# Two of the six model-column blocks of the first tile's layer 1 computed in one pass of 512 tokens instead of two passes of 256

## The chip, the core and the metric

One NeuronCore of one Trainium2 chip runs the whole program. The metric is the device time of one execution in microseconds (us), as a median of several runs. The engines are named as in the profile: PE (TensorE matmul), PEld (its weight loads), DVE (VectorE), ACT (ScalarE), POOL (GpSimd) and SP (the queue that issues most DMAs).

## What is computed

The reference has three stages, each feeding the next. Only what matters here is kept:

```python
y = _attn_ref(x, a, B, C)        # a chunked decay attention: batch 4, 8 heads, 768 tokens, head dim 32
x = y.transpose(0, 2, 1, 3).reshape(3072, 256)
h = np.maximum(np.maximum(x @ w1, x @ w2), x @ w3)      # layer 1: 256 -> 768
x = h @ w_out                                           # 768 -> 256
h = x @ w_in                                            # layer 2: 256 -> 2048
g = np.maximum(h, 0.0) + alpha * np.minimum(h, 0.0)
out = g @ w_out2                                        # 2048 -> 256
```

## The kernel before

**Tokens.** The 3072 tokens form 24 blocks of 128 (block r) and six tiles of 512 (tile t = blocks 4t to 4t+3). Attention is done block by block, the two layers tile by tile, and attention for later blocks is spread between the matmuls of the layers.

**Units.** The work of a layer is cut into units. One unit of layer 1 is one block f of 128 of the 768 hidden columns, over a number of tokens. `up1` (L664 to L682) makes three products (j = 0, 1, 2, for w1, w2, w3). Each is six matmuls (L652) into one of three PSUM buffers called `up`, because every operand is held as a high and a low part: two steps of the contraction, times high by high, low by high and high by low. ACT moves the first product out (L676), DVE takes the maximum with the second and the third (L678). ACT then makes the high part gh (L137) and POOL the low part gl (L138). The unit's way down (`down`, matmuls `acc<-gh,wo` and `acc<-gl,wo`, six in all) comes two units later (LAG = 2). A unit of layer 2 has one product of six matmuls, two DVE steps out of PSUM (L690, L691), then gh, gl and six matmuls down (`acc<-gh,vo`, `acc<-gl,vo`).

**Order of the phases.** Tile 0 layer 1, tile 1 layer 1, tile 0 layer 2, tile 2 layer 1, tile 1 layer 2, and so on. Tile 0's layer 1 is the first phase. Its units are taken in halves of 256 tokens, so that it can begin when attention blocks 0 and 1 are there:

```python
SPLIT, WHOLE = ((0, 256), (256, 256)), ((0, 512),)
ORDER = [(0, 0), (1, 0), (0, 1), (1, 1), (2, 0), (2, 1)]
        cut = [(f, *tokens[h]) for q, h in ORDER for f in (2 * q, 2 * q + 1)]
```

A pair (q, h) stands for the column blocks 2q and 2q+1 on token piece h of SPLIT. So the units are, in order: blocks 0 to 3 on tokens 0 to 255 (units 0 to 3), blocks 0 to 3 on tokens 256 to 511 (units 4 to 7), blocks 4 and 5 on tokens 0 to 255 (units 8 and 9), blocks 4 and 5 on tokens 256 to 511 (units 10 and 11). From unit 4 on all four attention blocks of tile 0 are done. Units 12 to 17 are tile 1's layer 1, units 18 to 33 tile 0's layer 2.

**Attention between the units.** A list `todo` of small steps is handed out at a rate (`quota`) worked out from the columns left until the next tile needs its blocks. For block r the steps on PE are: `att_t` (transposes, L400), `att_b` (products of C and B, L478, later L468), `att_y` (the output, L552 and L560) and `att_u` (the state, L511). ACT makes the decay matrix e by exponentials (`att_e`, L456) from a DMA of sums (`e<-cum_d`, L350), POOL masks it (L459), DVE multiplies it by the result of `att_b` (L483). The result of `att_y` goes into the next layer's input, high part by ACT (L569), low part by DVE (L570). Tile 1's first matmul needs block 7. In this text y7 means `att_y` of block 7, and so on.

**Weights.** 28 pieces of weights arrive by DMA (L163) and are turned from 64-bit words into two parts in four steps each, 112 steps in all: DVE L177, DVE L179, ACT L183, and DVE L185, which also lets ACT rebias the next piece (L170). In the first phase each unit hands out four such steps (pace 1). Afterwards `quota_w` spreads what is left over the units until the weights are needed.

**What orders the instructions.** In the first phase a scheduler of the language orders each engine's instructions. From tile 1 on (STRICT = 1) they stand in the order in which the program writes them. On every engine instructions are executed in order.

Of the kernel before, what the change touches and what calls it, by code (L numbers as in the profile page):

```python
# [27 lines left out]
NF1, NF2 = FF1 // P, FF2 // P  # L28
NT = BT * S // 512

SPLIT, WHOLE = ((0, 256), (256, 256)), ((0, 512),)
LATE = 4
PHASES = [(1, 0, SPLIT, 1), (1, 1, WHOLE, 0)]
for _t in range(NT - 2):
# [20 lines left out]
NPA = 2  # L55
SUMS = 0
WIDE = 18
ORDER = [(0, 0), (1, 0), (0, 1), (1, 1), (2, 0), (2, 1)]
BW, KW = 1, 3
WARM = 8  # L60
IDLE = 2
# [22 lines left out]
def fused(ctx: ExitStack, tc: tile.TileContext, x, a, B, C, w1, w2, w3, w_out, v_in, v_out, alpha, cst, out):  # L84
# [535 lines left out]
    def units_of(ph):  # L620
# [4 lines left out]
        else:  # L625
            cut = [(f, *tokens[h]) for q, h in ORDER for f in (2 * q, 2 * q + 1)]
        return [(f, o, n, (24 if layer == 1 else 12) * n, (4 * t + (o + n) // P) * (layer == 1),
# [494 lines left out]
```

## Time and profile before

| | us |
|---|---|
| median of 3 runs | 541.57 |
| lowest, highest | 541.23, 543.72 |
| profiled execution: its own time | 540.72 |
| profiled execution: span of its instructions | 539.0 |

The profile is of one execution. Its span runs from the first instruction to the last, and 1.72 us lie around it. Times in its rows are counted from the start of the span.

### The profile page before, as it was taken

What the parts mean: (1) busy time and instruction counts of PE and PEld (TensorE: products, weight loads), DVE (VectorE), ACT (ScalarE), POOL (GpSimd) and SP (SyncE); (2) the same over time, 40 slices, a digit from 0 to 9 for tenths busy, and PEclk for the clock granted to TensorE, in tenths of its full rate; (3) what the DMA queues carried; (4) which work ended last, traced back from release to release, by engine and by line L of the source; (5) the groups of instructions that cost most, each with busy time, mean ns of one, the idle gap of its engine ahead of it and who ended that gap; (6) DMA issues with size and microseconds to landing.
All of it is one profiled execution on the core that took longest, in us unless ns stands there. A gap on an engine that the chain in (4) does not pass through costs nothing.

```text
span 539.0 us, 9568 instructions
## 1 busy us (share of the span) xinstructions
PE 527.4 (98%) x3402; PEld 427.1 (79%) x3403; DVE 341.4 (63%) x596; ACT 254.1 (47%) x610; POOL 242.3 (45%) x267
## 2 busy tenths in 40 slices
PE   8898999999999999999999999999999999999997
PEld 4777888787788888888788888888877888778886
DVE  5887886789984547665347566345845736775453
ACT  6677774664653342432433424424242234766551
POOL 2143453443763433654433645422553352885550
PEclk9999999999999999999999999999999999999999
DMA  8978796687753762535663644634220200000024
GB/s 153 231 149 187 181 189 167 156 219 173 200 109 75 158 122 62 134 73 99 129 135 66 131 96 88 137 75 119 48 64 2 39 1 0 1 0 1 1 40 119
DMA packets 209344, 55.60 MB, mean 103 GB/s; under 512 B 159632, under 2 KB 201168, under 8 KB 209296
## 3 DMA queue, kind: packets, MB, share of 16 engines
q1 hardware_dynamic: 206928, 54.46, 45.9%
q10 hardware_dynamic: 2368, 0.52, 0.4%
q8 instruction: 27, 0.44, 0.4%
q14 instruction: 21, 0.17, 0.1%
HBM read 44.35 MB, written 10.62 MB: 102 GB/s over the span
## 4 chain that ended last, share of the span: by engine, by line
PE 82%; DVE 7%; ACT 3%; issue 3%; DMA 2%; POOL 1%; SPq 1%; ACTq 0%; DVEq 0%; POOLq 0%
PE up L652 43%; PE acc L652 27%; PE at L652 5%; PE at L539 1%; DVE v L179 1%; PE at L468 1%; POOL gl L138 1%; DVE g L678 1%; DMA xm<-in_x_dram 1%; PE at L536 1%; SPq L247 1%; DMA e<-cum_d 1%; PE up L977 1%; ACT e L451 1%; PE at L478 1%
## 5 line engine op out<-in xcount | busy, mean ns | idle before, releaser
L138 POOL TENSOR_TENSOR gl<-g,gh 128x512 fp32r<-128x512 f32 (+1 forms) x109 | 136.6, 1253 | 218.0 <-ACT gh L137 207.6
L652 PE MATMUL up<-xt,w 128*128 128x512 f32 (+1 forms) x777 | 168.5, 364 | 1.1 <-ACT xt L569 0.6
L137 ACT ACTIVATE gh<-g 128x512 fp32r<-128x512 f32 (+1 forms) x114 | 69.4, 609 | 186.3 <-DVE g L691 101.8
L652 PEld LDWEIGHTS up<-xt,w 128*128 128x128 f32 x777 | 132.5, 188 | 26.6 <-issue 2.2
L652 PE MATMUL up<-yt,vi 128*128 128x512 f32 x459 | 117.0, 389 | 0.0
L678 DVE TENSOR_TENSOR g<-up,g 128x512 f32<-128x512 f32 (+1 forms) x84 | 51.3, 611 | 77.2 <-PE up L652 75.6
L652 PEld LDWEIGHTS up<-yt,vi 128*128 128x128 f32 x459 | 86.0, 188 | 17.9
L652 PE MATMUL acc<-gh,vo 128*128 128x512 f32 x268 | 83.9, 394 | 0.0
L690 DVE TENSOR_SCALAR g<-up,alph 128x512 f32<-128x512 f32 x64 | 47.8, 747 | 38.0 <-PE up L652 36.3
L652 PEld LDWEIGHTS acc<-gh,vo 128*128 128x128 f32 x268 | 49.1, 188 | 10.4 <-issue 0.4
L652 PE MATMUL acc<-gl,vo 128*128 128x512 f32 x134 | 52.4, 391 | 0.2
L652 PE MATMUL acc<-gh,wo 128*128 128x512 f32 (+1 forms) x168 | 47.2, 365 | 0.3 <-ACT gh L137 0.2
L691 DVE SCALAR_TENSOR_TENSOR g<-up,g 128x512 f32<-128x512 f32 x64 | 44.3, 692 | 2.2
L451 ACT ACTIVATE e<-e,ncum 128x128 f32<-128x128 f32 x120 | 38.0, 388 | 0.0
L676 ACT ACTIVATE g<-up 128x512 f32<-128x512 f32 (+1 forms) x42 | 22.4, 534 | 27.1 <-PE up L652 16.3
L652 PEld LDWEIGHTS acc<-gh,wo 128*128 128x128 f32 x168 | 29.7, 189 | 6.1 <-DVE yt L719 0.5
L652 PE MATMUL acc<-gl,wo 128*128 128x512 f32 (+1 forms) x84 | 30.2, 360 | 0.0
L652 PEld LDWEIGHTS acc<-gl,vo 128*128 128x128 f32 x134 | 25.2, 188 | 6.4 <-POOL gl L138 1.0
L179 DVE SCALAR_TENSOR_TENSOR v<-st,v 128x512 uint32<-128x512 uint32 x28 | 24.6, 879 | 2.3 <-ACT st L170 0.7
L452 POOL TENSOR_SCALAR_AFFINE_SELECT e<-e 128x512 f32<-128x512 f32 x30 | 19.8, 659 | 7.9 <-ACT e L451 7.9
L170 ACT ACTIVATE st<-st 128x512 f32<-128x512 f32 x28 | 18.8, 671 | 2.0 <-DMA st<-in_moe_w_in_dram 1.0
L867 DVE SCALAR_TENSOR_TENSOR g<-g,rest,up 128x512 f32<-128x512 f32 x16 | 11.9, 747 | 11.9 <-ACT g L866 11.6
(192 smaller groups left out, 658.6 us busy)
## 6 DMA issues: line engine op xcount, KB each, us to landing
e<-cum_w SPq DMA_DIRECT2D x30, 256.0 KB, 4.4
st<-sc SPq DMA_DIRECT2D x60, 128.0 KB, 2.5
sc<-ts SPq DMA_DIRECT2D x52, 112.0 KB, 2.4
st<-in_moe_w_out_dram SPq DMA_DIRECT2D x11, 512.0 KB, 5.7
st<-in_moe_w_dram SPq DMA_DIRECT2D x9, 512.0 KB, 4.9
st<-in_moe_w_in_dram SPq DMA_DIRECT2D x8, 512.0 KB, 5.0
v<-sc SPq DMA_DIRECT2D x60, 64.0 KB, 2.2
out_dram<-st SPq DMA_DIRECT2D x20, 128.0 KB, 3.0
```

The lines of the kernel that those rows point to most:

```text
L137: nc.scalar.activation(dst_h, src, AF.Copy)
L138: engine.tensor_tensor(dst_l, src, dst_h, ALU.subtract)
L170: nc.scalar.activation(hi, hi, AF.Prelu, scale=2.0 ** -112, alpha=2.0 ** 32)
L179: nc.vector.scalar_tensor_tensor(v, hi, 3, v, ALU.logical_shift_left, ALU.bitwise_or)
L451: nc.scalar.activation(e[:, q, :], e[:, q, :], AF.Exp, bias=ncum[:, k, b, 4 * g + q:4 * g + q + 1])
L452: nc.gpsimd.affine_select(out=e, in_=e, pattern=[[0, 4], [1, P]], compare_op=ALU.is_ge, fill=0.0, base=0, channel_multiplier=-1)
L652: nc.tensor.matmul(acc, w, r, start=(first and i == 0), stop=(last and i == len(todo_) - 1), skip_group_check=True)
L676: nc.scalar.activation(g, p, AF.Copy)
L678: nc.vector.tensor_tensor(g, p, g, ALU.max)
L690: nc.vector.tensor_scalar(g, p, 0.0, alph[:, f:f + 1], ALU.min, ALU.mult)
L691: nc.vector.scalar_tensor_tensor(g, p, 0.0, g, ALU.max, ALU.add)
L867: nc.vector.scalar_tensor_tensor(g, g, rest[:, f:f + 1], h, ALU.mult, ALU.add)
```

## The change

```diff
-SPLIT, WHOLE = ((0, 256), (256, 256)), ((0, 512),)
+SPLIT, WHOLE = ((0, 256), (256, 256), (0, 512)), ((0, 512),)
-ORDER = [(0, 0), (1, 0), (0, 1), (1, 1), (2, 0), (2, 1)]
+ORDER = [(0, 0), (1, 0), (0, 1), (1, 1), (2, 2)]
```

Column blocks 4 and 5 of tile 0 become two units of 512 tokens (units 8 and 9 of the changed kernel) in place of four of 256. The first phase then has ten units, and tile 1's layer 1 is units 10 to 15, tile 0's layer 2 units 16 to 31. With two units fewer, the first phase hands out 40 weight steps in place of 48. The instructions that do not belong to these blocks stay the same, but several stand elsewhere.

The first place is on PE, behind the way down of unit 6. There `att_b` of block 6 (L478) and the transposes of block 7 (L400) stand. Names: `xt_304` and `xt_305` are tile 0's input, high and low. Before:

```order
L478 MATMUL at<-bc 64x128 x8
L400 MATMUL at<-ct,b 128x128
L400 MATMUL at<-ct,c 128x128
L400 MATMUL at<-ct,cp 128x128
L652 MATMUL up<-xt_304,w_0_112 128x256 x2
L652 MATMUL up<-xt_304,w_1_113 128x256 x2
L652 MATMUL up<-xt_305,w_0_112 128x256 x2
```

Now:

```order
L478 MATMUL at<-bc 64x128 x8
L400 MATMUL at<-ct,b 128x128
L400 MATMUL at<-ct,c 128x128
L400 MATMUL at<-ct,cp 128x128
L552 MATMUL at<-cpt,u 64x64 x2
L560 MATMUL at<-e,xm_108 32x64 x5
L552 MATMUL at<-cpt,u 64x64 x2
L560 MATMUL at<-e,xm_108 32x64 x11
L652 MATMUL up<-xt_304,w_0_112 128x512 x2
```

Before, all 18 matmuls up of unit 9 and six down of unit 7 stood between these transposes and y6 (L552, L560). Now y6 follows directly, and the unit's matmuls come behind it.

The second place is on PE, at the end of the first phase, behind y7. `xt_947` and `xt_948` are tile 1's input. Before:

```order
L552 MATMUL at<-cpt,u 64x64 x8
L560 MATMUL at<-e,xm_109 32x64 x16
L511 MATMUL at<-xm_110,bp 32x128 x4
L652 MATMUL up<-xt_304,w_0_112 128x256 x2
L652 MATMUL up<-xt_304,w_1_113 128x256 x2
L652 MATMUL up<-xt_305,w_0_112 128x256 x2
```

Now:

```order
L552 MATMUL at<-cpt,u 64x64 x8
L560 MATMUL at<-e,xm_109 32x64 x16
L511 MATMUL at<-xm_110,bp 32x128 x4
L652 MATMUL up<-xt_947,w_0_112 128x512 x2
L652 MATMUL up<-xt_947,w_1_113 128x512 x2
L652 MATMUL up<-xt_948,w_0_112 128x512 x2
```

Before, a whole unit of tile 0 (unit 11), six matmuls down and `att_b` of block 8 stood between u7 (L511) and tile 1's first matmul. Now tile 1's first matmul is next, and `att_b` of block 8 comes 12 matmuls after it.

The third place is on ACT, at the same time: the exponentials of block 8 (L456) and the copies of y7 (L569). Before:

```order
L137 ACTIVATE gh<-g 128x256
L569 ACTIVATE xt_947<-at 128x128
L456 ACTIVATE e<-e,ncum 128x64 x8
L569 ACTIVATE xt_947<-at 128x128
L676 ACTIVATE g<-up 128x256
```

Now:

```order
L456 ACTIVATE e<-e,ncum 128x64 x7
L137 ACTIVATE gh<-g 128x512
L456 ACTIVATE e<-e,ncum 128x64
L569 ACTIVATE xt_947<-at 128x128 x2
L676 ACTIVATE g<-up 128x512
```

Both copies of y7 now stand behind all eight exponentials of block 8 and behind unit 9's gh.

On SP the sums of block 8 (`e<-cum_d`) are now issued ahead of a weight piece that came before them. From tile 1 on a few attention steps stand up to one unit later than before, and otherwise the order of PE is the old one to the end of the program.

## Rows read from the trace of the kernel before

**Rows 1.** The page: span, part 1 (busy us, share, instructions), part 4 by engine.
```profile
span 539.0 us, 9568 instructions
PE 527.4 (98%) x3402; PEld 427.1 (79%) x3403; DVE 341.4 (63%) x596; ACT 254.1 (47%) x610; POOL 242.3 (45%) x267
PE 82%; DVE 7%; ACT 3%; issue 3%; DMA 2%; POOL 1%; SPq 1%; ACTq 0%; DVEq 0%; POOLq 0%
```

**Rows 2.** Busy time by stretch: length, PE, PEld, DVE, ACT, POOL, clock, DMA.
```profile
62.80:82.90 20.10, 19.24 (x315) 16.85 (x313) 17.54 (x44) 15.91 (x55) 10.36 (x16) 1.00 0.85 174
82.90:118.20 35.30, 35.19 (x241) 28.21 (x238) 26.87 (x45) 21.27 (x52) 13.15 (x18) 1.00 0.72 185
...
124.00:156.00 32.00, 31.81 (x161) 25.32 (x160) 30.94 (x49) 15.53 (x35) 17.05 (x16) 1.00 0.65 162
```

**Rows 3.** Timeline of PE, units 8 to 11: start, length, instructions.
```profile
62.80 0.52 PE L652 MATMUL up<-xt,w 128*128 128x256 f32 x3
...
78.40 0.65 PE L560 MATMUL at<-e,xm 128*32 128x64 f32 x32
78.87 0.40 PE L511 MATMUL at<-xm,bp 128*32 128x128 f32 x8
79.20 2.42 PE L652 MATMUL up<-xt,w 128*128 128x256 f32 x18
81.46 0.40 PE L652 MATMUL acc<-gh,wo 128*128 128x256 f32 x2
...
81.82 0.40 PE L652 MATMUL acc<-gh,wo 128*128 128x256 f32 x2
...
82.27 0.67 PE L478 MATMUL at<-bc 64*64 64x128 f32 x16
82.87 4.42 PE L652 MATMUL up<-xt,w 128*128 128x512 f32 x18
```

**Rows 4.** The chain that ended last, in order of time: 18 matmuls of 512.
```profile
166.61 4.08 PE up L652 x18
```

**Rows 5.** Timeline, all engines: b6, its product with e, y6, b7.
```profile
67.84 0.67 PE L478 MATMUL at<-bc 64*64 64x128 f32 x16
...
69.09 0.74 DVE L483 TENSOR_TENSOR e<-at,e 128x256 f32<-128x256 f32 x2
...
71.78 0.34 PE L552 MATMUL at<-cpt,u 32*64 32x64 f32 x8
...
74.83 0.85 PE L478 MATMUL at<-bc 64*64 64x128 f32 x16 [0.75 <-DVE xt L570]
```

**Rows 6.** Timeline of SP and ACT: DMA issues up to block 8's sums, its exponentials.
```profile
68.83 2.24 SPq L233 DMA_DIRECT2D b<-in_B_dram  x1
...
73.78 1.12 SPq L350 DMA_DIRECT2D e<-cum_d  x2
...
79.41 2.10 ACT L456 ACTIVATE e<-e,ncum 128x64 f32<-128x64 f32 x8 [0.23 <-DMA e<-cum_d]
81.41 0.26 ACT L569 ACTIVATE xt<-at 128x128 fp32r<-128x128 f32 x1
```

**Rows 7.** Weight steps: L179 (ns min/median/max); L177, L185 by shape, 118 to 160 us.
```profile
L179 DVE SCALAR_TENSOR_TENSOR v<-st,v x28: 676/693/1610, 10.1 to 152.9; 128x512 uint32<-128x512 uint32 x28
...
L177 DVE TENSOR_SCALAR v<-st 128x512 uint32<-128x512 uint32 x6 | 3.1, 510 | 0.0
L185 DVE TENSOR_TENSOR vi<-v,vi 128x512 fp32r<-128x512 f32 x3 | 2.3, 776 | 0.0
```

**Rows 8.** Tile 0's layer 2: weight loads down with idle, one gl and its matmul.
```profile
L652 PEld LDWEIGHTS acc<-gl,vo 128*128 128x128 f32 x24 | 4.5, 188 | 1.9 <-POOL gl L138 1.0
...
130.31 1.30 POOL L138 TENSOR_TENSOR gl<-g,gh 128x512 fp32r<-128x512 f32 x1 [2.47 <-ACT gh L137]
...
131.67 0.50 PE L652 MATMUL acc<-gl,vo 128*128 128x512 f32 x1
```

## The prediction

> **What bounds the kernel now.** I first read the page. PE is busy for 527.4 of 539.0 us, and 82% of the chain that ended last lies on PE [rows 1]. So time is won where PE does less or waits less, and an engine beside it counts only where PE waits for it. The change acts in the stretch of units 8 to 11, 62.80 to 82.90 us of the span, so I read the busy time by stretch next. PE is busy for 19.24 of 20.10 us there, and DVE with 17.54 us and ACT with 15.91 us have 2.5 and 4.2 us to spare [rows 2]. Two later stretches get weight steps that the first phase gives up. In tile 1's layer 1 (82.90 to 118.20) DVE is busy for 26.87 of 35.30 us. In tile 0's layer 2 (124 to 156) it is busy for 30.94 of 32.00 us, which is 97%, while PE hardly waits [rows 2]. There DVE is nearly a second bound.
>
> Then I read PE's timeline for the places where work for attention and work for the layers meet, and the timelines of ACT and SP beside it [rows 3, 5, 6]. They show which distances on PE hide something now.
>
> **Part 1: fewer, wider matmuls.** Four units of 24 matmuls over 256 columns become two units of 24 over 512. In the row of unit 11, the 18 matmuls up start at 79.20 and the next instruction at 81.46: 2.26 us, 125.6 ns each. Of the way down, three start from 81.46 to 81.82, 120 ns each [rows 3]. At 512 columns 18 take 4.08 us, 226.7 ns each [rows 4]. So 72 x 125.6 + 24 x 120 = 11.92 us become 48 x 226.7 = 10.88 us: **-1.04 us**. If all the narrow ones took 120 ns it would be 11.52 - 10.88 = -0.64 us. I take -1.04, since unit 11 is one of the units that go.
>
> A rule speaks against this term. The Trainium skill, page "TensorE: Matmul & The Clock Gate", section "Back-to-back issue gap", gives the distance of isolated matmuls at full clock as columns over 2.4 GHz plus about 2.5 ns. By it two of 256 need only some 2.5 ns more than one of 512, and this part would give about 0.1 us (an estimate from that page). The rows differ: they show 240 to 251 ns for two of 256 against 226.7 ns, so I keep the term from the rows.
>
> Fused moves out of PSUM and fused gh and gl save some DVE, ACT and POOL time. I cost this at nothing, since these engines have spare time in that stretch [rows 2] and PE doesn't wait for these steps: way down comes two units later.
>
> **Part 2: y6 directly behind att_b of block 6.** Now 3.94 us of PE's work lie between the start of b6 (67.84) and y6 (71.78), mostly unit 9 up. DVE's product, which y6 needs, starts 1.25 us and ends 1.99 us after the start of b6 [rows 5]. In the new order only b6 and the three transposes, about 0.9 us, lie between. If DVE were as quick as now, PE would wait about 1.1 us. In the new DVE order a maximum over 512 and an L179 (0.69 us at the median [rows 7]) stand ahead of the product, behind the same matmuls. I take **+1.2 us**. Bounds: 0.3 us, if DVE is free and only its 0.74 us for the product counts against part of the transposes, and 2.2 us, if a long L179 (1.61 us [rows 7]) falls there. Behind the waiting y6 stand unit 9 and with it all of PE.
>
> **Part 3: the wait at b7.** PE waits there 0.75 us for the copies of y6 to free PSUM [rows 5]. In the new order the same work lies between y6 and b7 (u7 and six matmuls, now twice as wide, in place of u7 and eight), and five exponentials stand ahead of the copies on ACT. I leave it as it is: **0**, from -0.75 (gone) to +0.9 (it doubles).
>
> **Part 4: tile 1's first matmul directly behind u8.** Now from 79.20 to 82.87 unit 11, six matmuls down and b8 lie between the end of att_u of block 8 and tile 1, 3.67 us [rows 3]. They hide the copies of y7, and even a detour: the second copy (81.41) waits behind the eight exponentials of block 8 (2.10 us), and these wait for a DMA that lets them start at 79.41 [rows 6]. In the new order none of that cover is left; the hidden work is done after tile 1's first matmuls instead, so only the wait counts. When is PE there? Now u8 ends at 79.20 [rows 3]. Up to that point the new order has 36 wide matmuls up and 12 narrow ones down, 9.60 us, in place of 54 and 18 narrow ones, 8.94 us: 0.66 us more. With the 1.2 us of part 2, y7 ends at about 80.7 and u8 at 81.0. The exponentials need block 8's sums. Their DMA is issued at 73.78 [rows 6]. In the new order it goes ahead of a weight piece, but behind the load of b for block 9, which waits for the transposes of block 7 (68.83 now, behind L400), and these come 1.7 us later. The two nearly cancel, and the load of b took 2.24 us to issue anyway [rows 6]. If the exponentials start near 78 us, they and gh (0.6 us) are done by 80.8, and the copies of y7, two on ACT of 0.26 us each [rows 6], end at about 81.4. So PE waits **+0.4 us**. Bounds: 0 (ACT is early and u8 covers the copies) and +3.4 us (below, the rival).
>
> **Part 5: eight weight steps later.** Steps done when tile 0's layer 2 is through with them stay 112. Working the shares through `quota_w`, tile 1's layer 1 hands out 27 steps instead of 23 and the first twelve units of layer 2 27 instead of 23. Four steps are one piece: L177 0.51 + L179 0.69 + L185 0.78 = 2.0 us of DVE [rows 7]. In tile 1's layer 1 DVE has 8.4 us to spare [rows 2], so **0** there, up to +1. In layer 2 it has 1.06 us to spare between 124 and 156. Already now PE's weight loads stand idle for 1.0 us for gl [rows 8], as at 131.67, when PE starts 0.06 us after gl has ended (130.31 + 1.30) [rows 8]. gl follows gh, and gh DVE's two steps. So up to 2.0 us of DVE may reach PE. Early units get little of it, and in between there is slack of one to two us at other units. I take **+0.7 us**, from 0 to 2.0.
>
> Of L179 the row shows 676 to 1610 ns, with a median of 693 [rows 7]. The Trainium skill, page "SBUF — State Buffer", section "Who interferes with whom", says that a DVE instruction with two SBUF inputs and a GpSimd instruction that reads SBUF block each other for the whole instruction. By that rule an L179 that meets a gl on POOL takes the long time, which agrees with the maximum of that row. At 1.61 us a piece would cost 2.9 us of DVE, and the upper bound of this part would be 2.9 us.
>
> **Sum.** -1.04 + 1.2 + 0 + 0.4 + 0 + 0.7 = **+1.3 us**. The profiled execution took 540.72 us (539.0 of span and 1.72 around it), so the new one would take about 542.0. The median of the three runs, 541.57, stands 0.85 above it, and by it the forecast is **542.9 us**, +0.24%.
>
> **Rivals.**
>
> *Nothing new waits.* DVE and ACT have 40 steps to do in place of 48 in the first phase, they keep up, and only part 1 counts, with 0.64 to 1.04 us: 540.5 to 540.9. For it: DVE's spare 2.5 us in that stretch [rows 2]. Against it: the 1.99 us from b6 to the end of the product [rows 5] cannot fit in 0.9 us. Chance 0.20.
>
> *The lighter first phase removes waits.* All of PE's 20.10 - 19.24 = 0.86 us idle in that stretch [rows 2] goes too, with part 1 and nothing of the rest: -1.9, 539.7. If the 1.0 us of waits for gl in layer 2 [rows 8] went as well, it would be -2.9, 538.7. For it: 8 steps less on DVE and ACT. Against it: y6 has lost its cover. Chance 0.09.
>
> *Slower: the sums of block 8 land late and tile 1 waits for them.* Place: ACT, L456 ahead of L569. If the DMA slips by the 1.7 us of the transposes, the exponentials start at 81.1, end at 83.2, gh follows with 0.6 and the copies with 0.5: tile 1 starts at 84.4 instead of 81.0, a wait of 3.4 us in place of 0.4. Sum +4.3: 545.9. It decides as soon as the sums land after about 78.2 us, when ACT can no longer be through at 81. For it: now they let ACT start only at 79.41, with DMA engines busy for 85% of the stretch [rows 2, 6]. Against it: half a megabyte of weights no longer goes ahead of them. Chance 0.16.
>
> *The change does not do what it says* is no rival here: the rows on PE show the wider matmuls in place.
>
> **How the numbers follow.** The forecast has 0.55, the rivals 0.20, 0.09 and 0.16. The forecast's own range is 541.6 to 544.4, from the parts' bounds taken two at a time. To leave out no more than 2 in 10, the range reaches down to the gain alone, 540.4, and up part of the way to the slow rival, 545.4. Half a per cent is 2.7 us, about what a measurement of this kernel can tell from no change: faster means below 538.9, slower above 544.3. Faster gets 0.07 (most of the second rival), slower 0.19 (the slow rival and the top of the forecast's range), same 0.74.
>
> **What would show it.** In the new profile, 512-column rows at 226.7 ns in units 8 and 9 (part 1). A wait of PE at L552 or L560 for DVE L483 near 70 us (part 2). A wait at L478 for L570 near 74 us (part 3). A wait of PE at L652 for ACT L569 at tile 1's first matmul near 81 us, with L456 just ahead of L569 on ACT (part 4). DVE at 97% or more to about 158 us and PE waits for POOL gl above 1.0 us in tile 0's layer 2 (part 5). The prediction is wrong if PE does not wait at tile 1's first matmul, if that wait exceeds 2 us, or if layer 2 loses more than 2 us.

## The result, and the profile after

| | before | after |
|---|---|---|
| median, us | 541.48 (18 runs) | 544.73 (18 runs) |
| lowest, highest, us | 540.04, 543.72 | 543.54, 550.1 |
| profiled execution, us: its time, its span | 540.72, 539.0 | 544.61, 542.5 |

The ratio is 1.0065, with a 95% interval from 1.005 to 1.0081. The kernel became slower by 0.65%. The forecast was +0.24%, inside the range that reached to 545.4 us. Of the 3.9 us between the profiled executions 3.5 lie in the span and 0.4 outside it (2.11 us around the span instead of 1.72). The ratios in this text are of medians, each against the kernel before as it was run beside (541.0 to 541.5 us).

First the page of the kernel after (answers to [rows 1]), then its busy times by stretch (answers to [rows 2]):

```profile
span 542.5 us, 9456 instructions
PE 528.8 (97%) x3354; PEld 424.8 (78%) x3355; DVE 340.8 (63%) x592; ACT 253.1 (47%) x606; POOL 240.0 (44%) x265
```

```profile
62.80:82.90 20.10, 18.28 (x254) 13.58 (x253) 13.59 (x34) 13.76 (x50) 8.33 (x14) 1.00 0.79 149
82.90:118.20 35.30, 34.02 (x215) 27.41 (x214) 25.97 (x47) 19.04 (x44) 13.46 (x18) 1.00 0.68 171
124.00:156.00 32.00, 31.14 (x156) 23.96 (x155) 30.80 (x49) 16.70 (x36) 16.11 (x17) 1.00 0.70 177
```

PE is now idle for 1.8 us in the first of these stretches, 1.3 in the second and 0.9 in the third; before it was 0.9, 0.1 and 0.2. The view of waits of PE, 60 to 150 us, names what it waited for (total, times, longest; one row of 0.2 us left out):

```profile
PE at L468 <- DVE u L504: 1.3, 1, 1.3
PE up L652 <- ACT xt L569: 1.2, 1, 1.2
PE acc L652 <- POOL gl L138: 0.6, 1, 0.6
PE at L552 <- DVE e L483: 0.4, 1, 0.4
PE at L332 <- DVE bc L409: 0.3, 1, 0.3
...
```

Before, this view had one row, the 0.75 us at L478 of [rows 5]. Now PE's timeline through units 8 and 9 up to tile 1's first matmul (answers to [rows 3, 5]), and ACT's in front of it (answers to [rows 6]):

```profile
65.97 3.46 PE L652 MATMUL up<-xt,w 128*128 128x512 f32 x14
69.27 0.40 PE L652 MATMUL acc<-gh,wo 128*128 128x256 f32 x2
...
70.94 0.27 PE L400 MATMUL at<-ct,cp 128*128 128x128 f32 x1
71.58 0.33 PE L552 MATMUL at<-cpt,u 32*64 32x64 f32 x4 [0.36 <-DVE e L483]
...
72.91 0.96 PE L652 MATMUL up<-xt,w 128*128 128x512 f32 x3
...
75.05 0.67 PE L478 MATMUL at<-bc 64*64 64x128 f32 x16
...
75.95 3.02 PE L652 MATMUL up<-xt,w 128*128 128x512 f32 x12
78.80 0.40 PE L652 MATMUL acc<-gh,wo 128*128 128x256 f32 x2
...
79.60 0.47 PE L552 MATMUL at<-cpt,u 32*64 32x64 f32 x16
...
80.48 0.40 PE L511 MATMUL at<-xm,bp 128*32 128x128 f32 x8
```

```profile
79.28 1.78 ACT L456 ACTIVATE e<-e,ncum 128x64 f32<-128x64 f32 x7 [2.26 <-DMA e<-cum_d]
80.97 0.61 ACT L137 ACTIVATE gh<-g 128x512 fp32r<-128x512 f32 x1
81.49 0.33 ACT L456 ACTIVATE e<-e,ncum 128x64 f32<-128x64 f32 x1
81.72 0.42 ACT L569 ACTIVATE xt<-at 128x128 fp32r<-128x128 f32 x2
```

Tile 1 starts at 82.03, behind a wait of 1.15 us for the last of these rows. The place that no step of the prediction had is att_b of block 9, in tile 1. PE there:

```profile
100.61 2.90 PE L652 MATMUL up<-xt,w 128*128 128x512 f32 x12
104.78 0.71 PE L468 MATMUL at<-st,v 128*128 128x256 f32 x4 [1.27 <-DVE u L504]
```

To see where the time went I set the starts of equal work side by side, read from PE's timelines: the first matmul of unit 8, the first matmul of tile 1's way down, att_b of blocks 9 (b9), 10 and 12. From unit 8 to tile 1's way down it took 35.79 us before and 36.29 after (+0.50), from there to b9 4.20 and 5.66 (+1.46), from b10 to b12 40.96 and 42.36 (+1.40). Behind b12 the distance stays at 3.5 us to the end. So about a seventh of the loss in the span lies in the stretch that the change rewrites, and the rest behind it. These stretches, like all those below, are read from one execution of each kernel. Executions of one kernel lie 1.5 to 6.6 us apart ("after": 543.54 to 550.1), so a stretch explains the profiled execution, and only the ratio speaks for the kernel.

### The profile page after: what moved, and what is told of

Same layout as the page of the kernel before. It is cut to its first block, busy times and chain, and to the rows that moved or that the text cites. A ratio compares the mean times of both kernels' runs of the same rounds, so it can differ in the third digit from the quotient of the medians.

```text
span 542.5 us, 9456 instructions
## 1 busy us (share of the span) xinstructions
PE 528.8 (97%) x3354; PEld 424.8 (78%) x3355; DVE 340.8 (63%) x592; ACT 253.1 (47%) x606; POOL 240.0 (44%) x265
## 4 chain that ended last, share of the span: by engine, by line
PE 75%; DVE 9%; ACT 5%; DMA 5%; issue 2%; SPq 1%; POOL 1%; ACTq 0%; DVEq 0%; POOLq 0%
PE up L652 40%; PE acc L652 25%; PE at L652 5%; DMA e<-cum_d 2%; PE at L539 1%; DVE v L179 1%; PE at L468 1%; DMA b<-in_B_dram 1%; ACT e L456 1%; DVE g L678 1%; DMA st<-in_moe_w_in_dram 1%; ACT gh L137 1%; PE at L536 1%; DVE g L690 1%; DVE v L177 1%
## 5 line engine op out<-in xcount | busy, mean ns | idle before, releaser
L138 POOL TENSOR_TENSOR gl<-g,gh 128x512 fp32r<-128x512 f32 (+1 forms) x107 | 134.6, 1258 | 225.5 <-ACT gh L137 214.6
L652 PEld LDWEIGHTS up<-xt,w 128*128 128x128 f32 x741 | 130.4, 189 | 28.3 <-ACT xt L569 2.7
L691 DVE SCALAR_TENSOR_TENSOR g<-up,g 128x512 f32<-128x512 f32 x64 | 44.2, 691 | 2.2
L179 DVE SCALAR_TENSOR_TENSOR v<-st,v 128x512 uint32<-128x512 uint32 x28 | 22.8, 815 | 1.8 <-ACT st L170 1.2
L570 DVE TENSOR_TENSOR xt<-at,xt 128x128 fp32r<-128x128 f32 x48 | 11.8, 285 | 13.9 <-ACT xt L569 13.8
```

The source lines that it names most:

```text
L138: engine.tensor_tensor(dst_l, src, dst_h, ALU.subtract)
L179: nc.vector.scalar_tensor_tensor(v, hi, 3, v, ALU.logical_shift_left, ALU.bitwise_or)
L570: nc.vector.tensor_tensor(xt[t][1][:, g, o], yp[g], xt[t][0][:, g, o], ALU.subtract)
L652: nc.tensor.matmul(acc, w, r, start=(first and i == 0), stop=(last and i == len(todo_) - 1), skip_group_check=True)
L691: nc.vector.scalar_tensor_tensor(g, p, 0.0, g, ALU.max, ALU.add)
```

## The experiments

Two shifts come with the change besides the wide units. Tile 1 starts with 58 weight steps done instead of 66. And attention, also handed out unit by unit, is one step behind: worked through `quota`, tile 1 starts with 0.99 of a step owed and 92 steps left, and before the change with 0.85 owed and 91 left. The first shift was in the prediction, the second was not. My first theory was that the late weight steps cost both losses behind the first phase; the rival was that the late attention step costs the one at b9. The first four runs put back one, the other, both, or moved the wide units.

**Weight steps back.**

```diff
-                owing[1] = pace or quota_w(at)
+                owing[1] = 2 * pace if pace and n == 512 else pace or quota_w(at)
```

> The change, but the two whole units hand out 8 weight steps each instead of 4, so that the first phase is through with 66 steps when tile 1 starts, as before the change; the order on PE stays that of the change. Theory 'late weight steps' (they alone cost what is lost behind the first phase, 1.4 us at att_b of block 9 and 1.4 us in tile 0's layer 2): about 541.9 us, and the wait at block 9 is gone. Rival 'late attention step' (the change also hands out one step of attention less in its first phase, because it has two units fewer; that brings the state update of block 8 and att_b of block 9 closer together on PE): the 1.3 us wait at block 9 stays; only the 1.4 us of layer 2 may go: 543.3 us. If neither counts: 544.7 us.

Measured: 546.86 us, ratio 1.0096 (1.008 to 1.0111): slower than the change, and above all three expected values. From b10 to b12 it took 40.55 us, so layer 2's loss went. The wait at b9 stayed. And the wait in front of tile 1 grew to 2.7 us. The timeline shows what stands there (SP, ACT, PE), and a row of the busy times what followed:

```profile
76.02 0.53 SPq L163 DMA_DIRECT2D st<-in_moe_w_out_dram  x1
77.06 0.37 SPq L163 DMA_DIRECT2D st<-in_moe_w_in_dram  x1
...
80.69 0.35 ACT L456 ACTIVATE e<-e,ncum 128x64 f32<-128x64 f32 x1 [2.99 <-DMA e<-cum_d]
...
83.44 0.73 PE L652 MATMUL up<-xt,w 128*128 128x512 f32 x2 [2.72 <-ACT xt L569]
```

```profile
84.00:88.00 4.00, 4.00 (x15) 2.84 (x13) 0.00 (x0) 1.67 (x3) 0.66 (x1) 0.57 0.49 104
```

Two weight pieces are issued right behind the sums of block 8, where the kernel after issues one, and the exponentials start at 80.69 instead of 79.28. After the wait of 2.72 us the granted clock is 0.57 from 84 to 88 us, so PE ran for most of that time at the lower of its two levels, 1.2 GHz. That the second piece is what makes the sums land later is likely from this order; no run moved that piece alone. The rival had both places behind the first phase right and the first theory only layer 2, and neither foresaw the price in front of tile 1.

**Attention step back.**

```diff
                 fixed.enter_context(tc.manual_schedule())
+                owed += 0.79
```

> The change, but 0.79 of a step of attention is added to what is owed when tile 1 starts. From the third unit of tile 1 on, the instructions on PE then stand in the order of before; the weight steps stay late (58 at the start of tile 1). Theory 'late attention step': the wait of 1.3 us at att_b of block 9 goes, 543.2 us if the loss in layer 2 is due to the weight steps, 541.9 us if that loss comes of the order too. Rival 'late weight steps': no change, 544.7 us.

Measured: 543.67 us, ratio 1.0048 (1.0031 to 1.0064). The wait at b9 is gone: 4.10 us from the way down to b9. From b10 to b12 it took 43.13 us, so layer 2 keeps its loss.

**Both back** (both edits above).

> The change with both put back: 8 weight steps for each whole unit, and 0.79 of a step of attention at the start of tile 1. What is left of the change is the wider units themselves and the seam in front of tile 1. If the losses behind the first phase come from these two shifts, 541.9 us (the 0.5 us of the first phase and the seam over the kernel before). If they come from something else that the wide units do, 543 to 545 us.

Measured: 545.88 us, ratio 1.0078 (1.0063 to 1.0092), above both expected values. Behind the first phase nothing is lost any more (4.10 us to b9, 40.99 from b10 to b12), but unit 8 to tile 1's way down took 37.12 us, with 2.1 us of wait in front of tile 1. The profiled execution, 542.99 us, was the fastest of the six; what the slower ones lost besides is not in a trace.

**Wide units in the middle** (both edits, 0.617 in place of 0.79 since the remainder is another).

```diff
-ORDER = [(0, 0), (1, 0), (0, 1), (1, 1), (2, 2)]
+ORDER = [(0, 0), (1, 0), (0, 1), (2, 2), (1, 1)]
```

> As the last one, but the two whole units stand ahead of the last pair of halves (blocks 2 and 3 over the second 256 tokens), not at the end of the first phase, so that tile 1 starts behind two narrow units as before the change. Theory 'the place costs, not the width' (product of block 6 and copies of block 7 lose their cover because the whole units come last): the gain of 0.6 to 1.0 us of the wider matmuls is left, 540.5 to 541.2 us. Rival 'the width costs' (attention steps come six to a whole unit and stand on PE directly behind one another wherever it stands): 541.9 us or more.

Measured: 542.63 us, ratio 1.0024 (1.0008 to 1.004), as the rival had it. No wait in front of tile 1, 41.04 us from b10 to b12. The place in front of tile 1 costs most of what "both back" lost, but moving the units does not bring the gain of their width either. What takes its place was not followed up; one wait in the first phase is 0.55 us at L552 for the product with e.

The next runs go at the two shifts from the other side, in the kernel before, where no unit is wide.

**The kernel before with a late attention step.**

```diff
-                own = quota(at)
+                own = 0.0 if (f, o, n) == (5, 256, 256) else quota(at)
```

> The kernel before, all blocks in halves, but the last unit of the first phase hands out no step of attention, so that tile 1 starts one step behind, and PE's order from there on is that of the changed kernel. The weight steps stay where they were (66 at the start of tile 1). Theory 'one late attention step costs 1.4 us at att_b of block 9' (the distance from the state update of block 8 to att_b of block 9 shrinks from 24 to 18 wide matmuls): a wait of 1.3 us at L468 for DVE, 542.8 us. Rival 'the wait needs the wide units or the late weight steps too': no such wait, 541.4 us.

Measured: 544.32 us, ratio 1.0059 (1.0036 to 1.0082). From the way down to b9 7.28 us instead of 4.20, and 40.53 from b10 to b12. One late step of attention alone costs nearly as much as the whole change. The profiled execution, 542.73 us, is one of the two fastest of the six (542.52 to 546.81).

**The kernel before with late weight steps.**

```diff
-                owing[1] = pace or quota_w(at)
+                owing[1] = pace / 2 if pace and f >= 4 else pace or quota_w(at)
```

> The kernel before, all blocks in halves, but the four units of blocks 4 and 5 hand out 2 weight steps each instead of 4, so that tile 1 starts with 58 steps done, as with the change; the order of attention stays that of before. Theory 'late weight steps cost tile 0's layer 2': 1.4 to 2.0 us more from att_b of block 10 to att_b of block 12, with PE's weight loads waiting for gl, and 542.8 to 543.4 us if the lighter first phase gives nothing back; with a shorter first phase (its DVE had 2.5 us to spare) as low as 542. Rival 'layer 2 does not feel them': 541.4 us or less.

Measured: 543.88 us, ratio 1.0052 (1.0036 to 1.0069). 4.10 us to b9, 43.80 from b10 to b12 (+2.84), and the stretch to the way down is 0.47 us shorter. The waits from 82.9 to 166 us, of PE and of its weight loads:

```profile
PE acc L652 <- POOL gl L138: 1.3, 2, 0.6
...
PEld acc L652 <- POOL gl L138: 4.1, 8, 1.1
```

**The weight steps in tile 1 instead** (with the attention step back).

```diff
-                owing[1] = pace or quota_w(at)
+                owing[1] = 31 / 24 if n_ph == 1 else pace or quota_w(at)
```

> The change, with the order of attention put back as in the run with 0.79 of a step added, and the 8 missing weight steps handed out in tile 1's layer 1 (31 there instead of 27, 58 at its start, 89 at its end as before the change), where DVE has spare time. Theory: the first phase keeps its lighter load (the wait in front of tile 1 stays near 1 us and not 2 to 3), block 9 has its distance, and layer 2 has the load of before: 541.4 to 542.0 us. Rival 'DVE in tile 1's layer 1 cannot take 8 more': a wait there of 1 us or more, 543 us or more.

Measured: 545.6 us, ratio 1.0081 (1.0067 to 1.0095). The theory fell. b9 is in time (4.25 us), but b10 to b12 took 44.05 us although layer 2 hands out the steps of before. DVE comes into layer 2 late. ACT and DVE at the end of tile 1:

```profile
115.67 1.27 ACT L451 ACTIVATE e<-e,ncum 128x128 f32<-128x128 f32 x4
116.84 0.62 ACT L183 ACTIVATE vi<-v 128x512 fp32r<-128x512 f32 x1
...
117.49 0.84 DVE L185 TENSOR_TENSOR vi<-v,vi 128x512 fp32r<-128x512 f32 x1 [1.79 <-ACT vi L183]
```

A piece goes from DVE to ACT and back. L183 stands behind gh and four exponentials on ACT, and DVE waits 1.79 us at L185. Time to spare over a stage is no time to spare at a handover. That this wait is what layer 2 then loses was not tested by a run of its own; what the profile shows there is PE waiting three times for gl, 1.9 us in all.

**Attention spread over the wide units** (half of a unit's steps behind its second product, as in later phases).

```diff
-                if n_ph >= STRICT and layer == 1:
+                if layer == 1 and n == 512:
```

> The change, but the two whole units hand out half of their attention steps after their second group of matmuls up and half at their end, so that on PE 6 wide and 6 narrow matmuls stand between the scores of block 6 and its product again. Nothing else is moved. Theory 'the product of block 6 lost its cover': the 1.0 us wait at L552 for the product goes, and 0.5 to 1.0 us with the split that it made: 543.7 to 544.2 us, if the wait in front of tile 1 does not take it back. Rival 'it only moves the wait to tile 1's first matmul, which depends on the sums of block 8 from memory': that wait grows from 1.2 to about 2.2 us, 544.7 us.

Measured: 544.88 us, ratio 1.0069 (1.0054 to 1.0083), no change. In the profile the wait of 0.36 us for the product of block 6 is gone (the 1.0 us that I expected to go is another one, at 41 us, which the kernel before has too), and that in front of tile 1 is 0.8 us; the stretch to the way down took 35.46 us, 0.83 less than with the change. b9 and layer 2 lose as with the change (5.67 and 42.49 us). The timed runs show no gain of 0.8 us, so whether it holds in general stays open.

The last question was why one late step is so dear. PE's row at b9 names DVE L504 as what ended the wait, and so does the chain. But the view of waits of SP's queue shows something else, 90 to 106 us, first of the kernel after, then (88 to 102 us) of the kernel before:

```profile
SPq L425 <- DVE v L179: 1.5, 1, 1.5
```

```profile
SPq L163 <- DVE v L179: 1.7, 1, 1.7
```

It is the same wait, for DVE to be through with one of the three buffers `st`. Before, the load of the next weight piece (L163) stands in it, behind block 9's loads. After, the weight piece stands ahead of them, because with attention one step late the weight step that issues it is handed out between the stores and the loads of block 9's turned b and c, and the load L425 waits. SP after, and PE at b9 of "before, late attention step", where the last L425 is issued at 102.01:

```profile
92.11 2.43 SPq L395 DMA_DIRECT2D sc<-ts  x4
94.65 0.53 SPq L163 DMA_DIRECT2D st<-in_moe_w_in_dram  x1
...
96.95 0.42 SPq L423 DMA_DIRECT2D v<-sc  x1
98.95 0.31 SPq L425 DMA_DIRECT2D st<-sc  x1
...
101.74 0.43 SPq L425 DMA_DIRECT2D st<-sc  x1
```

```profile
105.17 0.71 PE L468 MATMUL at<-st,v 128*128 128x256 f32 x4 [2.89 <-DVE v L179]
```

Here the row names another step of DVE, L179. But b9 starts 3.16 us behind the issue of the last L425 here and 3.04 us behind it in the kernel after (101.74 to 104.78), and these loads took 2.1 to 2.7 us from issue to landing.

**Block 9's loads ahead of the weight piece.** The edit only holds back the issue of L163 between the stores and the loads of block 9; PE, DVE and ACT keep their order.

```diff
-        i = len(staged)
+        i = held.append(1) or len(wq) if held else len(staged)
...
-            used = 6 + (r % NB > 0)
+            used, _ = 6 + (r % NB > 0), held.extend([0] * (r == 9))
...
-            yield lambda: att_l(r + 2), 0
+            yield lambda: (att_l(r + 2), release()), 0
```

> The change, with one difference, on the queue of SP: the load of one weight piece (L163) that stood between the stores and the loads of block 9's turned b and c stands behind those loads. PE, DVE and ACT keep their order. Theory 'the late attention step costs what it costs because a weight piece gets ahead of block 9's loads and takes one of the three st buffers that they need' (the first load into st then waited 1.6 us on SP): the loads land 1.6 to 2 us earlier, the wait of 1.3 us at att_b of block 9 goes, 543.3 us, less what the later weight piece costs in layer 2. Rival 'the distance on PE from the state update of block 8 (L504) is too short': the wait for DVE L504 stays, 544.7 us.

Measured: 543.21 us, ratio 1.003 (1.0009 to 1.005). From the way down to b9 4.23 us; from b10 to b12 43.24. The timeline of SP, DVE and PE there:

```profile
97.26 0.37 SPq L425 DMA_DIRECT2D st<-sc  x1
...
100.64 0.39 SPq L163 DMA_DIRECT2D st<-in_moe_w_in_dram  x1
...
103.38 0.92 DVE L504 SCALAR_TENSOR_TENSOR u<-u,dec_w 128x64 f32<-128x64 f32 x1
...
103.40 0.64 PE L468 MATMUL at<-st,v 128*128 128x256 f32 x4
```

L425 is issued 1.69 us earlier, and b9 starts 0.02 us after L504 has started, not behind its end. So it never waited for L504: in the kernel after that row was only the last event ahead of b9. The distance on PE is the same 18 matmuls. The rival has fallen; the queue and the buffers `st` are the cause at b9. In this execution the same thing comes back one stage on: a weight piece (L163 at 136.10) stands ahead of the loads of block 11, their first L425 is issued at 140.17, and PE waits at b11:

```profile
146.70 0.71 PE L468 MATMUL at<-st,v 128*128 128x256 f32 x4 [1.11 <-DMA c<-in_C_dram]
```

So about 1.1 of the 2.28 us by which layer 2 is longer here than before are a wait for loads, and not for DVE.

**Sums of block 8 one block earlier.**

```diff
-        if 0 < r < NR - 1:
-            cum_rows(r + 1)
+        for q in {6: (7, 8), 7: ()}.get(r, (r + 1,) if 0 < r < NR - 1 else ()):
+            cum_rows(q)
```

> The change, but the sums of block 8 are loaded along with those of block 7, one block earlier. Theory 'tile 1's first matmul waits for the copies of y7 because the exponentials of block 8 stand ahead of them and wait for these sums': the wait of 1.2 us in front of tile 1 goes, to 0.3 us or less, 543.6 us. Rival 'ACT is not through in time anyway, or the wait only moves to block 9': 544.7 us.

Measured: 544.07 us, ratio 1.0042 (1.0021 to 1.0064). The last exponentials of block 8 start at 76.95, and tile 1 follows u8 without a wait:

```profile
76.95 0.59 ACT L456 ACTIVATE e<-e,ncum 128x64 f32<-128x64 f32 x2
...
80.79 3.07 PE L652 MATMUL up<-xt,w 128*128 128x512 f32 x12
```

Unit 8 to the way down took 35.00 us, 0.79 less than before the change. The other two losses are there (5.62 and 42.55 us).

**All of it put back** (weight steps in the wide units, attention step, spread, early sums).

> The change with all of it put back: the 8 weight steps in the whole units, the 0.79 of a step of attention, attention spread over the whole units, and the sums of block 8 loaded one block earlier. Theory 'the gain of the wider matmuls is real and the losses are those three': 540.4 to 541.0 us, faster than both kernels by little. Rival 'eight more steps in the first phase make DVE and ACT late there whatever the sums do' (both runs that put them back had 2 us or more of wait in front of tile 1): 542 to 544 us.

Measured: 541.77 us, ratio 1.0014 (0.9992 to 1.0035): no difference from the kernel before. 4.10 us to b9 and 40.96 from b10 to b12, as before. Unit 8 to the way down took 36.09 us, 0.30 more than before. The time lies between the two theories. The waits of PE, 64 to 102 us:

```profile
PE at L478 <- DVE xt L570: 0.4, 1, 0.4
PE up L652 <- DVE xt L570: 0.4, 1, 0.4
PE up L652 <- ACT xt L569: 0.3, 1, 0.3
```

The first is the wait at b7 that the kernel before has, the other two stand at tile 1's first matmuls (82.56 and 84.11). So a part of the wait in front of tile 1 is there again, in spite of the early sums. This profiled execution (542.58 us) is 1.8 us longer in its span than the one before, and 1.54 of them lie ahead of unit 8, outside the stretches, where the granted clock was 0.79 from 8 to 16 us.

**The same, with the weight steps spread evenly over the first phase.**

```diff
+                owing[1] = 1.25 * pace or quota_w(at)
```

> As the last run (attention step put back, attention spread over the whole units, sums of block 8 early), but the missing weight steps are spread over all ten units of the first phase, 5 each instead of 4, and not put on the two whole units; 66 are done when tile 1 starts, as before the change. Theory 'the extra steps hurt where they pile up in front of tile 1': 540.4 to 541.2 us, faster than the last run. Rival 'DVE has no room for them in the first phase, wherever they stand': 541.8 us or more.

Measured: 541.67 us, ratio 1.0012 (0.9998 to 1.0027), between the two expected values and no different from the last run. Unit 8 to the way down took 36.84 us; here PE waits for 1.4 us at a transpose (L400) for POOL's cp (L359), in unit 9. No version beat the kernel before.

The stretches in one table (us; steps: weight steps done at tile 1's start; without the two runs whose first phase has another order):

| kernel | steps | attention | unit 8 to way down | to b9 | b10 to b12 | ratio |
|---|---|---|---|---|---|---|
| before | 66 | in time | 35.79 | 4.20 | 40.96 | 1 |
| before, late attention step | 66 | late | 35.45 | 7.28 | 40.53 | 1.0059 |
| before, late weight steps | 58 | in time | 35.32 | 4.10 | 43.80 | 1.0052 |
| after | 58 | late | 36.29 | 5.66 | 42.36 | 1.0065 |
| spread | 58 | late | 35.46 | 5.67 | 42.49 | 1.0069 |
| early sums | 58 | late | 35.00 | 5.62 | 42.55 | 1.0042 |
| loads first | 58 | late, loads ahead | 35.77 | 4.23 | 43.24 | 1.0030 |
| attention back | 58 | in time | 35.76 | 4.10 | 43.13 | 1.0048 |
| steps back | 66 | late | 39.62 | 6.16 | 40.55 | 1.0096 |
| both back | 66 | in time | 37.12 | 4.10 | 40.99 | 1.0078 |
| steps in tile 1 | 58 | in time | 36.77 | 4.25 | 44.05 | 1.0081 |
| all | 66 | in time | 36.09 | 4.10 | 40.96 | 1.0014 |

Whoever reads down "to b9" and "b10 to b12" sees two causes apart: b9 is late where the attention step is late and the loads were not moved, and layer 2 is long where 58 steps are done when tile 1 starts. "Steps in tile 1" has caught up before layer 2 begins and is longest there; its loss has another path, the late DVE.

## Why the prediction was right and wrong

The stretch from unit 8 to tile 1's way down holds the same work in both kernels. Here is PE's time in it, each row of the timeline taken to the start of the next, less the wait in brackets:

| us | before | after |
|---|---|---|
| the changed units, up and down: 96 matmuls of 256 columns, 48 of 512 | 12.79 | 11.98 |
| the way down of units 6 and 7 | 1.61 | 1.60 |
| 54 matmuls up of tile 1 | 13.19 | 12.67 |
| attention's matmuls | 7.45 | 8.23 |
| waits | 0.75 | 1.81 |
| sum | 35.79 | 36.29 |

**Part 1 (wide matmuls, -1.04)** was right: the gain is 0.81 us, between its two bounds. Both prices were too low, because both come from unbroken rows. 14 wide matmuls take from 65.97 to 69.27 and 12 from 75.95 to 78.80, 236 and 238 ns each, not the 226.7 of [rows 4], and groups of two and three take more. But the narrow ones stand in such broken groups too: 12.79 us in place of 11.92.

**Part 2 (y6 behind b6, +1.2)** was right in size, by half for another reason. y6 starts 0.64 us after the last transpose instead of right behind it, which is the wait that was forecast, at half its size. And it takes from 71.58 to 72.91, where the undivided y7 takes 0.88 us (79.60 to 80.48): 0.45 us more because it is done in four groups, which no part had.

**Part 3 (b7, 0)** came out at its lower bound: the wait of 0.75 us is gone.

**Part 4 (the seam, +0.4)** had the right mechanism, and the early sums showed it: the wait is 1.15 us, and it goes with them. The exponentials started at 79.28, not near 78. The reason that I gave against the slow rival, that fewer weights are on their way with the sums, fits what the two runs with the weight steps back show: 2.1 to 2.7 us of wait.

The four together were forecast at +0.56 us, and the stretch took 0.50 more. That is right in sum, and in part by luck: -0.81, +1.05, -0.75 and +1.15 make +0.64. Two terms that no part had nearly settle the rest: a new wait of 0.30 us at L332 in unit 8, and tile 1's matmuls up, which are 0.52 us shorter.

**Part 5, tile 1's layer 1 (0)** is the step that failed in its mechanism. It said that DVE has 8.4 us to spare there, so nothing is lost. DVE was not needed: it is busy for even less there than before. What was lost, 1.46 us, is a load queued behind a weight piece on SP, and it came of a shift that the prediction did not count at all, the late step of attention. I followed what the two lost units hand out in weight steps and not what they hand out in attention. The order of instructions showed b9 closer to y8; I took that for a move without a price.

**Part 5, layer 2 (+0.7, 0 to 2.0)** had the mechanism right and was too small: +1.40 us here, and 2.2 and 2.8 in "attention back" and "before, late weight steps", where PE's weight loads wait 3.5 and 4.1 us for gl in place of the 1.0 of [rows 8]. ("Loads first" has 2.3, of which about 1.1 is the wait at b11.) DVE is busy for 30.80 of 32.00 us. One place in the timeline of all engines:

```profile
135.14 1.29 POOL L138 TENSOR_TENSOR gl<-g,gh 128x512 fp32r<-128x512 f32 x1 [1.75 <-ACT gh L137]
...
135.36 1.62 DVE L179 SCALAR_TENSOR_TENSOR v<-st,v 128x512 uint32<-128x512 uint32 x1
...
137.68 0.69 DVE L691 SCALAR_TENSOR_TENSOR g<-up,g 128x512 f32<-128x512 f32 x1
...
138.48 0.63 ACT L137 ACTIVATE gh<-g 128x512 fp32r<-128x512 f32 x1 [0.84 <-DVE g L691]
...
139.19 1.28 POOL L138 TENSOR_TENSOR gl<-g,gh 128x512 fp32r<-128x512 f32 x1 [2.76 <-ACT gh L137]
...
140.53 0.50 PE L652 MATMUL acc<-gl,vo 128*128 128x512 f32 x1 [0.63 <-POOL gl L138]
```

L179 runs beside a gl on POOL and takes 1.62 us, against 0.68 without one. DVE's last step out of PSUM (L691) comes later by it, and gh, the next gl and PE follow. This agrees with the Trainium skill, page "SBUF — State Buffer", section "Who interferes with whom", which has such a pair on DVE and GpSimd block each other. Such a meeting is not new: between 118 and 160 us the kernel before has two long L179 as well (1.42 and 1.12 us), the kernel after two of 1.62. So it is one link of this wait and not by itself what the change costs.

**Outside the span**, 0.4 us that no part had.

**The rivals and the range.** "Nothing new waits" is out. The slow rival named the right place at the seam and the wrong size (1.15 us, not 3.4). That the lighter first phase gives time back was no whole case, but it is there: 0.47 us in "late weight steps", where no unit is wide. Of the three signs that were to show the prediction wrong none came: PE waits at tile 1's first matmul, for less than 2 us, and layer 2 loses less than 2. Still, the loss is 2.5 times the forecast (3.25 us between the medians, not 1.3). The measured 544.73 lies above the forecast's own range (541.6 to 544.4) and above its line for "slower" (544.3), to which it gave 0.19. It is inside 545.4 only because the range was drawn toward the slow rival, and it came there by b9 and by twice the forecast in layer 2: that the range held is luck.

Why does the wider form not pay even with everything put back? The weight steps that the two units gave up have to go somewhere, and in layer 2 DVE has no room for them. In the first phase they bring waits back: with 66 steps and all else in place ("all") the stretch took 36.09 us, with 1.04 us of waits for the copies `xt` at b7 and in front of tile 1, and with 58 ("early sums") 35.00 us, with one wait of 0.36 us. That the eight steps make these waits is likely from the difference, but the two runs also differ in the spread and in the attention step; this was not separated.

## What to carry to other kernels

When work is handed out unit by unit, fewer units shift everything that is handed out, so count each list and not only the one that you think of. The row that ended a wait may be only the last event before it: move the suspect alone, here one DMA on its queue, and see whether the wait follows. An engine's idle time over a stage says nothing about a step that goes from one engine to another and back; look at what stands ahead of it on both. And take the prices of two forms from rows that are broken up alike.

## What the hardware showed

After PE had stood for 2.72 us ("steps back") the granted clock was 0.57 from 84 to 88 us. The length of the wait alone does not settle it: after 2.89 us ("before, late attention step", b9) the clock was 1.00 in every two microseconds from 104 to 112, and after 2.12 us ("both back") 1.00 from 84 to 92; with a wait of 1.15 us (after) it stayed at 1.00 over 82.9 to 118.2. What decides stays open. It also differs between executions where the wait is the same: behind 0.95 us at L552 near 41 us the clock was 0.50 from 42 to 44 us in the kernel after and 1.00 there before. Unit 8 started at 62.83 and 62.80 us all the same.

A wide matmul cost 236 to 238 ns in groups of 12 and 14 behind attention's small ones, and 226.7 ns in a group of 18 behind other wide ones (88.41 to 92.49 in the kernel after).

The time around the span was 2.1 to 2.2 us in the kernel after and in five others with wide units, and 1.7 to 1.9 in the rest, "both back" and "all" among them. What sets it stays open.
